# One level of Strassen's scheme for the down projection of two token chunks, and a scale's matmul moved later

## The chip, the cores and the metric

The kernel runs on one core of one Trainium2 chip. The metric is the device time of a whole execution in microseconds (us). Names of engines in the profile: PE is TensorE (PEld its weight loads, which overlap PE), DVE is VectorE, ACT is ScalarE, POOL is GpSimd, SP is the engine that starts most transfers. "Lnnn" is a line of that kernel's own source, so the same operation has other line numbers in the kernel before and in the changed one.

## The reference, cut to what matters

A layer of 2048 tokens and width 1024: layer norm, a dilated local attention and its output projection, then layer norm and a gated feed-forward block with 3584 inner features. The change is in the last step, `h @ w_down`.

```
h  = x + A(layernorm(x))                  # attention, cut
def B(x, w_gate, w_up, w_down):
    g = x @ w_gate                        # (2048, 1024) @ (1024, 3584)
    u = x @ w_up
    return (g * u) @ w_down               # (2048, 3584) @ (3584, 1024)
h2 = h + B(layernorm(h))
```

## The kernel before

The tokens are worked in four chunks of 512. Chunks 0 and 1 go through the feed-forward block one by one. Chunks 2 and 3 go through gate and up together, in 14 "paired blocks", which already use one level of Strassen's scheme there (seven products where the plain way has eight). For that the weights are multiplied by a power of two, so that sums in float16 keep their digits. The power comes from the sum of all absolute values of the gate and up weights: ScalarE sums rows, VectorE adds the row sums, and a matmul with a tile of ones adds over the partitions. `make_scale` does the last two steps at once, ahead of chunk 2's output projection `wo_ln2(2)`:

```python
def make_scale():
    row = small.tile([128, 1], F32, tag="l1row")
    nc.vector.tensor_reduce(row[:], l1[:], mybir.AxisListType.X, ALU.add)
    ...                                                    # cut: rowb = row in bf16
    nc.tensor.matmul(ps[:], lhsT=ones[:], rhs=rowb[:].to_broadcast((128, TC)), start=True, stop=True)
    ...                                                    # cut: five small VectorE operations make s and 1/s
...
hT = ffn1(1, lnT2)
make_scale()
bg.finish(atts[2])
l2, hs2 = wo_ln2(2)
```

The down projection of chunks 2 and 3 is the plain one. `h23` holds the 56 tiles of h (28 feature tiles for each of the two chunks). TensorE makes 4 token tiles x 28 products for each half of the output columns and each chunk; the last group is done tile by tile, its fourth tile in two pieces.

```python
for c, hs in ((2, hs2), (3, hs3)):
    hT = [h23[2 * f + c - 2] for f in range(NF)]
    for hf in range(2):
        ffn2(c, hf, hT, hs)          # 4 tiles x 28 matmuls of 128x512, then 4 additions and stores
```

## Time and profile before

| | before |
|---|---|
| median of the first three runs | 799.41 us (798.01 to 801.58) |
| span of the profiled run | 798.9 us |
| PE, DVE, ACT busy in it | 785.1, 529.2, 304.4 us |
| start of the down projection of chunks 2 and 3 ("the seam") | 698.78 us |
| from the seam to the end | 100.1 us |

A share of busy time says which engine is short of time on average; what a stage is worth is read from the wait that ends last in it. Here TensorE has almost no waits, so each hole in it counts in full. The prediction shows the profile's lines.

### The profile page before, as it was taken

The numbers are of one execution on the slowest core, as the hardware profiler recorded it, in microseconds if no ns is written. First come the engines' busy times: TensorE is split into PE (matmuls) and PEld (weight loads), VectorE is DVE, ScalarE is ACT, GpSimd is POOL, SyncE is SP. The second block draws the span as 40 slices with busy tenths as digits, with TensorE's granted clock in tenths as the row PEclk, the third lists the DMA queues.
The fourth block names the chain that finished last, engine by engine and source line by source line (L and its number), as shares of the span: only waits on it lengthen the run. The fifth ranks groups of instructions, "written<-read, shape, count | busy, mean of one in ns | idle before, by whom it ended". The sixth has DMA issues, their size and how long they took to land.

```text
span 798.9 us, 9984 instructions
## 1 busy us (share of the span) xinstructions
PE 785.1 (98%) x3732; PEld 364.7 (46%) x3802; DVE 529.2 (66%) x606; ACT 304.4 (38%) x649; POOL 150.7 (19%) x160
## 2 busy tenths in 40 slices
PE   8999999999999999999999899999999999999998
PEld 5544444444444444444444344444444444444445
DVE  6629999999899998999989753724444444301111
ACT  4627445313766641026666300025455455500000
POOL 0000000200000200002000010066876876400000
PEclk9999999999999999999999999999999999999999
DMA  7898693987955968767637466523233133556500
GB/s 262 258 234 200 172 268 92 288 249 196 336 189 187 299 228 224 235 236 232 199 107 236 158 174 248 158 80 106 59 100 106 55 104 109 175 191 200 169 27 27
DMA packets 190977, 143.28 MB, mean 179 GB/s; under 512 B 79184, under 2 KB 183760, under 8 KB 188880
## 3 DMA queue, kind: packets, MB, share of 16 engines
q1 hardware_dynamic: 187344, 120.61, 50.4%
q0 software_dynamic: 3584, 22.02, 8.1%
q8 instruction: 30, 0.49, 0.2%
q14 instruction: 19, 0.16, 0.1%
HBM read 114.29 MB, written 22.02 MB: 171 GB/s over the span
## 4 chain that ended last, share of the span: by engine, by line
PE 73%; DVE 22%; issue 2%; SPq 1%; DMA 1%; ACT 1%; DVEq 0%
PE acc L602 21%; PE pg L392 9%; PE pu L392 9%; PE pz L653 6%; PE py L653 6%; PE px L653 6%; PE wo L513 5%; DVE pv L475 4%; DVE prod L432 4%; PE ps L392 3%; PE accl L592 3%; PE pv L653 3%; DVE prod L434 2%; DVE oD L485 2%; DVE pv L483 2%
## 5 line engine op out<-in xcount | busy, mean ns | idle before, releaser
L392 PE MATMUL ps<-lnT,w_qkv 128*128 128x512 bf16 x721 | 159.0, 379 | 1.0 <-ACT sg L303 0.2
L392 PEld LDWEIGHTS <-w_qkv 128*128 128x128 bf16 x736 | 71.9, 98 | 86.3 <-issue 0.5
L392 PE MATMUL pu<-lnT,w_wu 128*128 128x512 bf16 x438 | 105.1, 379 | 0.6
L392 PE MATMUL pg<-lnT,w_wg 128*128 128x512 bf16 x440 | 105.1, 379 | 0.4
L602 PE MATMUL acc<-w_wd,gs 128*128 128x512 bf16 x438 | 96.7, 379 | 0.5
L584 DVE TENSOR_TENSOR h<-acc,h 128x512 bf16<-128x512 f32 x28 | 17.4, 683 | 96.4 <-PE acc L602 96.4
L303 ACT CAST sg<-ps 128x512 bf16<-128x512 f32 x96 | 54.8, 590 | 53.2 <-PE ps L392 48.2
L475 DVE TENSOR_TENSOR pv<-vD,at 128x4096 bf16<-128x4096 bf16 x32 | 72.5, 2287 | 0.3
L432 DVE TENSOR_TENSOR prod<-qD,kD 128x4096 bf16<-128x4096 bf16 x32 | 72.3, 2284 | 0.1
L392 PEld LDWEIGHTS <-w_wu 128*128 128x128 bf16 x448 | 43.9, 98 | 52.8
L392 PEld LDWEIGHTS <-w_wg 128*128 128x128 bf16 x448 | 43.8, 98 | 52.9
L653 PEld LDWEIGHTS <-sw 128*128 128x128 f16 x448 | 43.8, 98 | 52.9
L602 PEld LDWEIGHTS <-gs 128*128 128x128 bf16 x448 | 43.8, 98 | 52.9
L513 PE MATMUL wo<-w_wo,oT 128*128 128x512 bf16 x251 | 57.2, 386 | 0.3
L653 PE MATMUL px<-lnT,ws 128*128 128x512 bf16 x211 | 52.6, 379 | 0.6
L573 ACT CAST us<-pu 128x512 bf16<-128x512 f32 x56 | 33.1, 591 | 50.5 <-PE pu L392 49.3
L653 PEld LDWEIGHTS <-ws 128*128 128x128 f16 x336 | 32.9, 98 | 39.6
L568 ACT CAST gs<-pg 128x512 bf16<-128x512 f32 x56 | 33.1, 590 | 45.9 <-PE pg L392 41.8
L182 ACT ACTIVATE rs<-mv,eps 128x1 f32<-128x1 f32 x32 | 9.5, 295 | 107.6 <-DVE mv L179 103.9
L487 POOL DMA_DIRECT2D od<-oD x4 | 2.2, 542 | 249.9 <-DVE oD L485 162.5
L632 POOL TENSOR_TENSOR sw<-ws 128x512 f16<-128x512 f16 x28 | 32.3, 1152 | 87.5 <-PE acc L602 46.4
L513 PEld LDWEIGHTS <-oT 128*128 128x128 bf16 x256 | 25.4, 99 | 31.4 <-issue 2.3
(140 smaller groups left out, 1027.9 us busy)
## 6 DMA issues: line engine op xcount, KB each, us to landing
w_wd<-in_B_w_down_dram SPq DMA_DIRECT2D x32, 896.0 KB, 5.8
w_wg<-in_B_w_gate_dram SPq DMA_DIRECT2D x14, 1024.0 KB, 6.5
w_wu<-in_B_w_up_dram SPq DMA_DIRECT2D x14, 1024.0 KB, 5.2
w_wo<-in_A_wo_dram SPq DMA_DIRECT2D x8, 1024.0 KB, 7.0
w_pair<-in_B_w_gate_dram SPq DMA_DIRECT2D x14, 512.0 KB, 3.8
w_pair<-in_B_w_up_dram SPq DMA_DIRECT2D x14, 512.0 KB, 4.9
w_qkv<-in_A_wqkv_dram SPq DMA_DIRECT2D x5, 1024.0 KB, 8.6
kd<-sg SPq DMA_DIRECT2D x32, 144.0 KB, 2.8
```

Of the source, the lines that this page charges most:

```text
L303: nc.scalar.copy(sg[:, HB:HB + TC], ps[:])
L392: nc.tensor.matmul(ps[:], lhsT=wt[:, ko, bass.ts(j, 128)], rhs=rhs[:, ko, :], start=(ko == 0), stop=(ko == KO - 1))
L432: nc.vector.tensor_tensor(prod[:, j], qD[:], kD[:, :, o:o + SUB], ALU.mult)
L475: nc.vector.tensor_tensor(pv[:, j], vD[:, :, o:o + SUB], at[:, w, None, :].to_broadcast((128, DH, SUB)), ALU.mult)
L513: nc.tensor.matmul(ps[:], lhsT=oTs[c][:, kk, t, :], rhs=wts["wo", c, hf][:, kk, :], start=(kk == 0), stop=(kk == KO - 1))
L568: nc.scalar.copy(gs[:], pg[:])
L573: nc.scalar.copy(us[:], pu[:])
L584: nc.vector.tensor_tensor(hs[t][:, cols], acc[:], hs[t][:, cols], ALU.add)
L592: nc.tensor.matmul(acc[:], lhsT=hT[f][:, bass.ts(t, 128)], rhs=wts["wd", c, hf, f // 7][:, f % 7, bass.ds(lo, n)], start=(f == 0), stop=(f ...
L602: nc.tensor.matmul(acc[t][:], lhsT=hT[f][:, bass.ts(t, 128)], rhs=wts["wd", c, hf, b][:, j, :], start=(f == 0), stop=(f == NF - 1))
L632: nc.gpsimd.tensor_tensor(sw[:, i, 0], a21, a22, ALU.add)
L653: nc.tensor.matmul(ps[:], lhsT=lhs[:, ko, :], rhs=rhs[:, ko, :], start=(fresh and ko == 0), stop=(ko == 3), skip_group_check=not fresh)
```

## The change

The intent is to save an eighth of TensorE's work in the down projection of chunks 2 and 3. The 2x2 scheme splits h by chunk (rows 1 is chunk 2, row 2 is chunk 3) and by even and odd feature tiles, and `w_down` by even and odd feature rows and by left and right output half. The sums and differences are made by VectorE, and the conversions to float16 ahead of them by VectorE and ScalarE. Since h needs a scale as well, ScalarE sums the absolute values of `w_down` (beside chunk 0's down projection) and of h (in the paired blocks). Separately, the gate and up scale's ones-matmul goes behind `wo_ln2(2)`. In the code `HA` are the four quarters of h in bf16, `HF` the same ones times the scale in float16, `b11` to `b22` the quarters of `w_down` (two tiles each, `dn_b11a` and `dn_b11b` in the profile), `t1` and `t2` sums of those, `S1` a sum of quarters of h, and `ps_x` and `ps_y` the PSUM banks (`dx` and `dy` in the profile). The names that begin with `hq` in the profile are the tiles that hold h. The diff, cut to its core:

```diff
 hT = ffn1(1, lnT2)
-make_scale()
+scale_gu.rows()                    # row sums, VectorE
+scale_d.rows()
 bg.finish(atts[2])
 l2, hs2 = wo_ln2(2)
+scale_gu.total()                   # ones-matmul and the five small operations
+scale_d.total()
 ...
-for c, hs in ((2, hs2), (3, hs3)):
-    ...
-        ffn2(c, hf, hT, hs)
+conv_down(down["b12"])             # VectorE: to f16, two tiles of 128x3584
+add_homes(t1v, Fv("b12"), Fv("b11"), ALU.subtract)      # t1, two sums of 128x3584
+scale_h.rows()
+conv_down(down["b21"])
+for q in range(4):
+    dprod(ps_x[q], q, HA["11"], fcells(down["b11"]), True)     # product 1: 14 matmuls for each q
+    if q == 1:
+        scale_h.total(ps_y[3])
+        ...                                                    # cut: inverse of both scales
+for q in range(4):
+    nc.scalar.activation(ps_y[q][:], ps_x[q][:], ACTF.Copy, scale=sh)
+for k in range(NP):                                            # 28 conversions on VectorE
+    to_f16(HF["22"][k], HA["22"][k], sh)
+    to_f16(HF["21"][k], HA["21"][k], sh)
+...                                                            # cut: 14 on ScalarE, S1 = 14 sums
+for q in range(4):
+    dprod(ps_x[q], q, HA["12"], fcells(down["b21"]), False)    # product 2
+    result(2, q, 0, ps_x[q], scale_d.inv, None)
+    if q == 2:
+        conv_down(down["b22"])
+...                                                            # cut: 28 differences on VectorE
+add_homes(t2v, Fv("b22"), t1v, ALU.subtract)                   # t2
+...                                                            # cut: product 3 (S1 x t1)
+for q in range(4):
+    dprod(ps_y[q], q, HF["11"], cells(t2h), False)             # product 4
+...                                                            # cut: products 5 and 6
+for q, lo, n in ((0, 0, 512), (1, 0, 512), (2, 0, 512), (3, 0, 256), (3, 256, 256)):
+    dprod(ps_y[q], q, HF["12"], fcells(down["b22"]), False, lo, n)    # product 7
+    result(2, q, 1, ps_y[q], inv, p5[q], lo, n)
```

Not shown are the loads of `w_down` for this stage, now made once and not once for each chunk, and the warm-up tile, which moves to another pool.

More of the change, by code (lines that the diff above doesn't have):

```diff
@@ L151 @@
     pair_at = len(stream)
-    for c in (2, 3):
-        stream_wd(c, 0)
-        stream_wd(c, 1)
     wts = {}
@@ L281 @@
     nc.scalar.preload_act_table_set("natural_log_exp_and_others")
-    warm = const.tile([128, 512], BF)
+    warm = t1k.tile([128, TC], BF, tag="t1k", name="warm")
     nc.vector.memset(warm[:], 0.0)
@@ L527, in wo_ln2, with __init__, add, rows @@
         return lnT, hs
-    l1 = const.tile([128, 56], F32)
     ones = const.tile([128, 128], BF)
     nc.vector.memset(ones[:], 1.0)
-    scale = {}
+    class Scale:
+        def __init__(self, name, n):
+            self.name, self.n = name, n
+            self.l1 = const.tile([128, n], F32, name="l1" + name)
+            self.rowb = const.tile([128, 1], BF, name="rowb" + name)
+        def add(self, k, src, junk):
+            nc.scalar.activation(junk, src, ACTF.Abs, accum_out=self.l1[:, k:k + 1])
+        def rows(self):
+            row = small.tile([128, 1], F32, tag="l1row", name="row" + self.name)
+            nc.vector.tensor_reduce(row[:], self.l1[:], mybir.AxisListType.X, ALU.add)
+            nc.vector.tensor_copy(self.rowb[:], row[:])
+        def total(self, ps=None):
+            ps = ps or psum.tile([128, TC], F32, tag="mm", name="l1ps" + self.name)
+            nc.tensor.matmul(ps[:], lhsT=ones[:], rhs=self.rowb[:].to_broadcast((128, TC)), start=True, stop=True)
+            tot = const.tile([128, 1], F32, name="tot" + self.name)
+            nc.vector.tensor_copy(tot[:], ps[:, 0:1])
+            eb = const.tile([128, 1], I32, name="eb" + self.name)
+            nc.vector.tensor_scalar(eb[:], tot[:].bitcast(I32), 0x7F800000, None, ALU.bitwise_and)
+            nc.vector.tensor_scalar(eb[:], eb[:], float(27 << 23), None, ALU.max)
+            sb = const.tile([128, 1], I32, name="sb" + self.name)
+            nc.vector.tensor_scalar(sb[:], eb[:], -1.0, float(266 << 23), ALU.mult, ALU.add)
+            ib = const.tile([128, 1], I32, name="ib" + self.name)
+            nc.vector.tensor_scalar(ib[:], eb[:], float(12 << 23), None, ALU.subtract)
+            self.s, self.inv = sb[:].bitcast(F32), ib[:].bitcast(F32)
@@ L535, in abs_sum @@
+    scale_gu, scale_d, scale_h = Scale("gu", 56), Scale("d", 56), Scale("h", 56)
     def abs_sum(c, b, j):
-        k = 28 * c + 4 * b + j
         wt = wts["wg" if c == 0 else "wu", c, b]
         junk = lnp.tile([128, 2, 512], BF, tag="ln", name=f"junk{c}_{b}_{j}")
-        nc.scalar.activation(junk[:], wt[:, bass.ts(j, 2), :], ACTF.Abs, accum_out=l1[:, k:k + 1])
-    def make_scale():
-        row = small.tile([128, 1], F32, tag="l1row")
-        nc.vector.tensor_reduce(row[:], l1[:], mybir.AxisListType.X, ALU.add)
-        rowb = small.tile([128, 1], BF, tag="l1rowb")
-        nc.vector.tensor_copy(rowb[:], row[:])
-        ps = psum.tile([128, TC], F32, tag="mm", name="l1ps")
-        nc.tensor.matmul(ps[:], lhsT=ones[:], rhs=rowb[:].to_broadcast((128, TC)), start=True, stop=True)
-        tot = const.tile([128, 1], F32)
-        nc.vector.tensor_copy(tot[:], ps[:, 0:1])
-        eb = const.tile([128, 1], I32)
-        nc.vector.tensor_scalar(eb[:], tot[:].bitcast(I32), 0x7F800000, None, ALU.bitwise_and)
-        nc.vector.tensor_scalar(eb[:], eb[:], float(27 << 23), None, ALU.max)
-        sb = const.tile([128, 1], I32)
-        nc.vector.tensor_scalar(sb[:], eb[:], -1.0, float(266 << 23), ALU.mult, ALU.add)
-        ib = const.tile([128, 1], I32)
-        nc.vector.tensor_scalar(ib[:], eb[:], float(12 << 23), None, ALU.subtract)
-        scale["s"], scale["inv"] = sb[:].bitcast(F32), ib[:].bitcast(F32)
@@ L559, in ffn1, with abs_sum_down, abs_sum_h @@
+        scale_gu.add(28 * c + 4 * b + j, wt[:, bass.ts(j, 2), :], junk[:])
+    def abs_sum_down(hf, b, j):
+        junk = lnp.tile([128, 512], BF, tag="ln", name=f"junkd{hf}_{b}_{j}")
+        scale_d.add(28 * hf + 7 * b + j, wts["wd", 0, hf, b][:, j, :], junk[:])
+    def abs_sum_h(n, k, ht):
+        junk = lnp.tile([128, 512], BF, tag="ln", name=f"junkh{n}_{k}")
+        scale_h.add(4 * n + k, ht, junk[:])
     def ffn1(c, lnT):
@@ L587, in ffn2 @@
     def ffn2(c, hf, hT, hs, between={}):
-        if c == NCH - 1 and hf == 1:
-            for t, lo, n in ((0, 0, 512), (1, 0, 512), (2, 0, 512), (3, 0, 256), (3, 256, 256)):
-                acc = psum.tile([128, n], F32, tag="mm", name=f"accl{t}_{lo}")
-                for f in range(NF):
-                    nc.tensor.matmul(acc[:], lhsT=hT[f][:, bass.ts(t, 128)],
-                                     rhs=wts["wd", c, hf, f // 7][:, f % 7, bass.ds(lo, n)],
-                                     start=(f == 0), stop=(f == NF - 1))
-                ffn2_store(c, t, hf, acc, hs, lo, n)
-            return
         acc = [psum.tile([128, 512], F32, tag="mm", name=f"acc{c}_{hf}_{t}") for t in range(4)]
@@ L604, in ffn2 @@
                                      start=(f == 0), stop=(f == NF - 1))
+                if c == 0:
+                    abs_sum_down(hf, b, j)
                 bg.step(0.86)
@@ L626, in weight_sums @@
         wt = wpool.tile([128, KO, 2, 256], F16, tag="w", name=f"ws_{n}")
-        nc.vector.tensor_scalar(wt[:], raw[:], scale["s"], None, ALU.mult)
+        nc.vector.tensor_scalar(wt[:], raw[:], scale_gu.s, None, ALU.mult)
         sw = wpool.tile([128, 2, 4, 4, 128], F16, tag="w", name=f"sw_{n}")
@@ L654, in product, with pair_block @@
                              stop=(ko == 3), skip_group_check=not fresh)
-    def pair_block(n, hts):
+    def pair_block(n, hts, sums=()):
         b11, b21, t1, t2, t3, t4, b22 = pair["b"]
-        wt, sw, inv = pair["a", n], pair["s", n], scale["inv"]
+        wt, sw, inv = pair["a", n], pair["s", n], scale_gu.inv
         gu = range(2)
@@ L683, in pair_block @@
             nc.scalar.activation(out[i][0], xb[i][:], ACTF.Copy, scale=inv)
+            for k in sums[2 * i:2 * i + 2]:
+                k()
         for i in gu:
@@ L758, with home, load_down, to_f16 @@
         h23 += [ht[:, k, :] for k in range(KO)]
+    wd_e = B_w_down.rearrange("(n e p) c -> e p n c", e=2, p=128)
+    NH = NF // 4
+    def home(pool, tag, name, dt=F16):
+        return pool.tile([128, KO, TC], dt, tag=tag, name=name)
+    def load_down(homes, e, hf):
+        for a, t in enumerate(homes):
+            nc.sync.dma_start(t[:, 0:NH, :], wd_e[e][:, bass.ts(a, NH), bass.ts(hf, 512)])
+    def to_f16(dst, src, sc, eng=nc.vector):
+        if eng is nc.scalar:
+            nc.scalar.activation(dst, src, ACTF.Copy, scale=sc)
+        else:
+            eng.tensor_scalar(dst, src, sc, None, ALU.mult)
+    def f16(ap):
+        return ap.bitcast(F16)
+    def conv_down(homes):
+        for t in homes:
+            to_f16(f16(t[:, 0:NH, :]), t[:, 0:NH, :], scale_d.s)
+    def cells(homes):
+        return [t[:, k, :] for t in homes for k in range(NH)]
+    down = {}
     for n in range(NP):
@@ L763 @@
                 load_pair(n + 2)
-        else:
-            state["limit"] = len(stream)
-            pump()
-        pair_block(n, h23[4 * n:4 * n + 4])
-    pump()
-    for c, hs in ((2, hs2), (3, hs3)):
-        hT = [h23[2 * f + c - 2] for f in range(NF)]
-        for hf in range(2):
-            ffn2(c, hf, hT, hs)
+            else:
+                names = ("b11a", "b12a", "b21a", "b21b", "b12b")
+                ws = {k: home(wpool, "w", "dn_" + k, BF) for k in names}
+                down["b11"] = [ws["b11a"], home(att, "oD", "dn_b11b", BF)]
+                down["b12"] = [ws["b12a"], ws["b12b"]]
+                down["b21"] = [ws["b21a"], ws["b21b"]]
+                load_down(down["b11"], 0, 0)
+                load_down(down["b12"], 0, 1)
+        else:
+            load_down(down["b21"], 1, 0)
@@ new lines @@
+        sums = [] if n == 0 else [
+            (lambda n=n, k=k: abs_sum_h(n - 1, k, h23[4 * (n - 1) + k])) for k in range(4)]
+        pair_block(n, h23[4 * n:4 * n + 4], sums)
+        if n == NP - 2:
+            conv_down(down["b11"])
+    HA = {"11": h23[0::4], "21": h23[1::4], "12": h23[2::4], "22": h23[3::4]}
+    for k in (3, 0, 2, 1):
+        abs_sum_h(NP - 1, k, h23[4 * (NP - 1) + k])
+    down["b22"] = [home(wpool, "w", "dn_b22a", BF), home(wpool, "w", "dn_b22b", BF)]
+    load_down(down["b22"], 1, 1)
@@ new lines, with add_homes, dprod @@
+    t1h = [home(lnTp, "lnT", "dn_t1a"), home(lnTp, "lnT", "dn_t1b")]
+    t2h = [home(att, "kD", "dn_t2a"), home(att, "vD", "dn_t2b")]
+    Fv = lambda k: [f16(t[:, 0:NH, :]) for t in down[k]]
+    def add_homes(dst, x0, x1, op):
+        for d, a0, a1 in zip(dst, x0, x1):
+            nc.vector.tensor_tensor(d, a0, a1, op)
+    ps_x = [psum.tile([128, TC], F32, tag="mm", name=f"dx{q}") for q in range(4)]
+    ps_y = [psum.tile([128, TC], F32, tag="mm", name=f"dy{q}") for q in range(4)]
+    def dprod(ps, q, lhs, rhs, fresh, lo=0, n=TC):
+        for k in range(NP):
+            nc.tensor.matmul(ps[:, bass.ds(lo, n)], lhsT=lhs[k][:, bass.ts(q, 128)], rhs=rhs[k][:, bass.ds(lo, n)],
+                             start=(fresh and k == 0), stop=(k == NP - 1), skip_group_check=not fresh)
@@ new lines, in fcells, with result @@
+    def fcells(homes):
+        return [f16(c) if c.dtype != F16 else c for c in cells(homes)]
+    def result(c, q, hf, ps, sc, other, lo=0, n=TC):
+        rows = (hs2 if c == 2 else hs3)[q]
+        cols = bass.ds(hf * 512 + lo, n)
+        nc.vector.scalar_tensor_tensor(rows[:, cols], ps[:, bass.ds(lo, n)], sc,
+                                       rows[:, cols] if other is None else other[:, bass.ds(lo, n)], ALU.mult, ALU.add)
+        nc.sync.dma_start(outf[bass.ds(c * TC + q * 128, 128), cols], rows[:, cols])
@@ new lines @@
+    conv_down(down["b12"])
+    t1v = [t[:, 0:NH, :] for t in t1h]
+    t2v = [t[:, 0:NH, :] for t in t2h]
+    add_homes(t1v, Fv("b12"), Fv("b11"), ALU.subtract)
[5 more added lines that the diff above has]
+            scale_h.total(ps_y[3])
+            inv = const.tile([128, 1], F32, name="inv_hd")
+            nc.vector.tensor_tensor(inv[:], scale_h.inv, scale_d.inv, ALU.mult)
+            inv = inv[:]
@@ new lines @@
+    sh = scale_h.s
+    for q in range(4):
+        nc.scalar.activation(ps_y[q][:], ps_x[q][:], ACTF.Copy, scale=sh)
+    HF = {k: [f16(a) for a in HA[k]] for k in HA}
+    for k in range(NP):
+        to_f16(HF["22"][k], HA["22"][k], sh)
+        to_f16(HF["21"][k], HA["21"][k], sh)
+    s1h = [t[:, 0:NH, :] for t in down["b11"]]
+    S1 = fcells(down["b11"])
+    for k in range(NP):
+        to_f16(HF["11"][k], HA["11"][k], sh, nc.scalar)
+    for k in range(NP):
+        nc.vector.tensor_tensor(S1[k], HF["21"][k], HF["22"][k], ALU.add)
@@ new lines @@
+    for q in range(4):
[3 more added lines that the diff above has]
+            conv_down(down["b22"])
+    for k in range(NP):
+        nc.vector.tensor_tensor(HF["21"][k], HF["11"][k], HF["21"][k], ALU.subtract)
+    for k in range(NP):
+        nc.vector.tensor_tensor(HF["11"][k], S1[k], HF["11"][k], ALU.subtract)
+    add_homes(t2v, Fv("b22"), t1v, ALU.subtract)
+    p5 = []
+    for q in range(4):
+        dprod(ps_x[q], q, S1, cells(t1h), True)
+        p = lnp.tile([128, TC], F32, tag="ln", name=f"dp5_{q}")
+        nc.scalar.activation(p[:], ps_x[q][:], ACTF.Copy, scale=inv)
+        p5.append(p)
@@ new lines @@
+    add_homes(Fv("b12"), Fv("b22"), Fv("b12"), ALU.subtract)
+    add_homes(Fv("b21"), Fv("b21"), t2v, ALU.subtract)
+    for q in range(4):
+        dprod(ps_y[q], q, HF["11"], cells(t2h), False)
+        nc.scalar.copy(ps_x[q][:], ps_y[q][:])
+    for k in range(NP):
+        to_f16(HF["12"][k], HA["12"][k], sh, nc.scalar)
+    for q in range(4):
+        dprod(ps_x[q], q, HF["21"], fcells(down["b12"]), False)
+        r = att.tile([128, TC], F32, tag=("lg", "t3")[q % 2], name=f"dr{q}")
+        nc.vector.tensor_tensor(r[:], p5[q][:], hs3[q][:, 512:1024], ALU.add)
+        result(3, q, 1, ps_x[q], inv, r)
@@ new lines @@
+    for k in range(NP):
+        nc.vector.tensor_tensor(HF["12"][k], HF["12"][k], HF["11"][k], ALU.subtract)
+    for q in range(4):
+        nc.vector.tensor_tensor(p5[q][:], p5[q][:], hs2[q][:, 512:1024], ALU.add)
+    for q in range(4):
+        dprod(ps_x[q], q, HF["22"], fcells(down["b21"]), False)
+        result(3, q, 0, ps_x[q], inv, None)
+    for q, lo, n in ((0, 0, 512), (1, 0, 512), (2, 0, 512), (3, 0, 256), (3, 256, 256)):
+        dprod(ps_y[q], q, HF["12"], fcells(down["b22"]), False, lo, n)
+        result(2, q, 1, ps_y[q], inv, p5[q], lo, n)
```

## The prediction

> **What bounds the kernel now.** I read the page's busy line and its row of slices first, then who TensorE waited for, then stretches of the span where something waits, then the groups with shapes kept apart.
>
> ```profile
> PE 785.1 (98%) x3732; PEld 364.7 (46%) x3802; DVE 529.2 (66%) x606; ACT 304.4 (38%) x649; POOL 150.7 (19%) x160
> PEclk9999999999999999999999999999999999999999
> ...
> PE l1ps L547 <- DVE rowb L545: 3.7, 1, 3.7
> PE ps L354 <- DMA w_qkv<-in_A_wqkv_dram: 1.4, 2, 0.9
> ```
>
> TensorE is busy 785.1 of 798.9 us: it is the bound everywhere, so only two things can shorten the kernel, fewer matmul columns or fewer holes. The list of TensorE's waits (last two lines) has one hole worth naming: the ones-matmul that sums the weight scale waits 3.7 us for VectorE's row sum, which stands behind the attention in VectorE's order. What that hole costs is seen in six stretches around it (columns: stretch, us, busy of PE, PEld, DVE, ACT, POOL, granted clock, DMA share, GB/s):
>
> ```profile
> 448.00:452.00 4.00, 0.35 (x2) 0.17 (x2) 3.59 (x5) 1.63 (x3) 0.40 (x1) 0.97 0.85 275
> 452.00:453.00 1.00, 1.00 (x4) 0.43 (x3) 0.65 (x5) 0.00 (x0) 0.16 (x1) 0.50 1.07 378
> 453.00:454.00 1.00, 1.00 (x4) 0.30 (x3) 0.03 (x1) 0.00 (x0) 0.00 (x0) 0.50 1.04 354
> 454.00:455.00 1.00, 1.00 (x4) 0.30 (x3) 0.00 (x0) 0.00 (x0) 0.00 (x0) 0.50 1.09 447
> 455.00:456.00 1.00, 1.00 (x6) 0.47 (x5) 0.48 (x1) 0.00 (x0) 0.00 (x0) 0.89 1.00 426
> 456.00:458.00 2.00, 2.00 (x11) 0.93 (x10) 0.96 (x3) 0.00 (x0) 0.00 (x0) 1.00 0.25 102
> ```
>
> After the hole TensorE is busy but granted 0.50 of its clock up to 455, then all of it. Half speed lasts some 3.46 us (0.03 x 4 / 0.5 = 0.24, then 3.00, then 0.11 / 0.5 = 0.22), which loses 1.73 us. The hole costs 3.65 + 1.73 = **5.4 us**.
>
> The stages that the change touches are the down projection of chunk 0 (302.8 to 351.2), the paired blocks (530 to 698.8), and the down projection of chunks 2 and 3 (from 698.8 on):
>
> ```profile
> 302.80:351.20 48.40, 48.14 (x221) 21.94 (x225) 45.99 (x39) 2.05 (x5) 0.00 (x0) 1.00 0.68 217
> 530.00:698.80 168.80, 168.06 (x770) 76.54 (x783) 75.85 (x123) 89.59 (x140) 117.11 (x104) 1.00 0.35 106
> 698.80:798.90 100.10, 96.48 (x469) 46.47 (x475) 12.47 (x22) 0.00 (x1) 0.00 (x0) 1.00 0.38 122
> ```
>
> In the last one VectorE (12.47 us) and ScalarE (0.00) are idle: the change spends this idle time. The unit prices are in these groups:
>
> ```profile
> L436 DVE TENSOR_TENSOR prod<-prod 128x2048 bf16<-128x2048 bf16 x16 | 19.6, 1223 | 0.4
> L627 DVE TENSOR_SCALAR ws<-w_pair,sb 128x4096 f16<-128x4096 bf16 x14 | 17.9, 1280 | 0.0
> L690 DVE TENSOR_TENSOR hq<-hq,up 128x512 bf16<-128x512 bf16 x24 | 8.5, 418 | 0.0
> L187 DVE TENSOR_SCALAR ln<-h,mv,rs 128x1024 bf16<-128x1024 bf16 x16 | 8.8, 551 | 2.7 <-ACT rs L183 2.4
> L539 ACT ACTIVATE junk<-w_wu 128x1024 bf16<-128x1024 bf16 x28 | 29.7, 1061 | 0.0
> ...
> 698.98 0.75 DVE L688 SCALAR_TENSOR_TENSOR up<-py,ib,p 128x512 bf16<-128x512 f32 x1 [0.97 <-PE py L653]
> 699.65 1.42 DVE L690 TENSOR_TENSOR hq_p<-hq_p,up 128x512 bf16<-128x512 bf16 x4
> ```
>
> A 16-bit sum of two tiles takes 0.418 us for 512 and 1.223 for 2048 elements, so 2.02 for the new 3584; one that follows another starts 0.08 us before its end (0.34 and 1.95 in a row). The f16 conversion of 4096 takes 1.28; between it and the 1024 of L187 the slope is 0.238 ns, so 3584 takes 1.16 (1.09 in a row) and 512 some 0.43 (0.355 in a row) at most. The last two lines, from the timeline, place VectorE at the seam: its h products end at 701.07, 2.3 us after the down projection has begun (698.78).
>
> **What the Trainium skill says.** "TensorE: Matmul & The Clock Gate", part 1, has the clock fall to one half after an idle window of about 3.4 us and come back after a busy one; its start-to-start for 512 columns is 215.7 ns warm. The trace agrees: 3.65 us idle, 3.46 us at 0.50, and matmuls every 0.216 us. "VectorE: DVE Perf Modes", what auto-detection checks, lets a one-source 16-bit op in SBUF run four wide, and caps a two-source one at two wide: 1280 ns against 2284 ns (group of L432) for 4096 elements agrees. "ScalarE: Activation LUTs", what ACT_TABLE_LOAD costs, gives 186 ns + 0.833 ns an element, each pointer operand 93 ns more, with back-to-back overlap of 93 ns: 1061 ns here for 1024 (1039 by the page). So 512 absolute values are an estimate of 0.61 us, plus the 0.19 of the accumulator read: 0.81 a pair in sequence, as 1.24 for 1024 now less 0.43. A conversion of 512 with a pointer scale is an estimate of 0.61 in a row.
>
> **Part by part.** *Removed:* the down projection has 2 chunks x 2 halves x 4 tiles x 28 = 448 matmuls of 512 columns. Seven products x 4 x 14 are 392. 56 x 0.216 = **12.1 us** less on TensorE. Its 14.7 MB of weight loads become 7.3, hidden before and after.
>
> *Moved:* the scale's matmul goes behind the output projection of chunk 2, by when VectorE has long made the row sum. Nothing else makes TensorE wait there: the projection takes 8 banks that ScalarE has emptied, VectorE starts on them at some 452.1 (TensorE would have the eighth at 461.9) and the next stage needs the third bank at 462.3, free at about 456. The whole 5.4 returns, less 0.2 for a second ones-matmul and 0.1 in rounding: **5.1 us**. Attention 3's result is stored from 451.6 whatever happens, and is used 16 us after it landed, so it doesn't take the gain.
>
> *Added on ScalarE:* 56 absolute sums beside the down projection of chunk 0, 56 x 0.81 = 45.4 us. It is free from 308 (earlier work waits for VectorE), so it ends at about 356 rather than 353 where its next copies start now; VectorE first needs one of them at 357.4. Free. In the paired blocks 4 x 0.81 = 3.2 us are added to 89.59 / 14 = 6.4 us, in a block of 12.06: about 9.6, free.
>
> *Added at the end,* in us from the seam T0. VectorE is in strict order: products to 2.3; convert b12 to 4.5; t1 = b12 - b11, two sums, to 8.5; row sum, 0.46 until the matmul can start as now. TensorE wants that at 28 x 0.216 = 6.05 and gets it at 8.9: **stall 2.85**. The first product ends at 15.2, the second at 27.3 (ScalarE's copies with the scale are ready from 12.6). VectorE then converts b21 and makes the scale (to 12.0), converts 28 tiles of h (9.9, to 22.0), makes S1 (14 x 0.34, to 26.8), three results (28.9), b22 (31.0) and the fourth result (31.7). The third product needs the first result's bank at 27.6: **stall 0.3**; it ends at 39.7. For the fourth VectorE has yet to do 28 differences (9.6, to 41.3) and t2 (two sums, the first at 43.3, the second at 45.2): **stall 3.7 + 0.4**. With cheaper small conversions (0.27) it is 1.7 less, so 3.3 on average. From there VectorE and ScalarE stay ahead: b12 and b21 differences to 53, one product lasts 12.1, and HF12 is ready 6 us before the last product. The tail is the same as now. Two holes of about 3 us may also throw the clock to one half, at 1.7 each: 2.85 is under the window and 3 to 4 is around it, so I charge 0.8 of one, 1.4.
>
> Sum at the end: 12.1 - 0.2 (scale of h) - 2.85 - 0.3 - 3.8 - 1.4 = 3.5. With 5.1: **8.6 us**, 799.4 - 8.6 = **790.8 us**.
>
> **The rivals.** (1) TensorE stays the bound all along: no stalls, 12.1 + 5.1 - 0.2 = 17.0, so 782.4, just over 2%. For it: order of work looks arranged for it (b22's conversion stands between results, ScalarE takes 28 of the conversions). Against it: two full-size sums stand ahead of the row sum, and 28 differences plus two sums in VectorE's order between products 3 and 4, 13.5 us plus leftovers against 12.1. (2) VectorE becomes the bound of the first half of the stage, small ops cost more than their slopes say, and both holes throttle: stalls 9 to 10 and 3.4 of half clock, nothing left of the 12.1; the moved matmul alone gives 794 to 795. (3) ScalarE's sums hold weight buffers or attention and make TensorE wait in chunk 0's stage: 45 us in 48 is tight, buffers come free 5 to 7 us later than now; against it, seven tiles of prefetch, each 6 us of TensorE. It would cost 1 to 4 us. (4) The gain of the moved matmul is hidden by a later wait; I find none.
>
> **Range and chances.** The moved matmul is nearly certain; the stalls' sum runs from 3 to 10 and the clock from 0 to 3.4. That gives 786 to 796. Over 2% faster means under 783.4, which needs nearly no stall: 0.06. Over 2% slower would need a mechanism that I don't see: 0.02.
>
> **What would show it.** The wait for the row sum gone at 448, no 0.50 clock there, chunk 2's projection starting 3.7 us earlier; one TensorE hole of about 3 us in the middle of the first product, before the ones-matmul, and one of 3 to 4 us ahead of the fourth product, released by VectorE; 392 matmuls at 0.216 us. Wrong if the holes are absent (then nearer 783), if the clock falls twice (794), or if TensorE waits in chunk 0's down projection or the paired blocks.

## The result, and the profile after

The changed kernel takes 787.83 us (median of 4 runs, 787.08 to 789.03), the kernel before 799.16 (4 runs, 798.01 to 801.58). The ratio is 0.9856, with a 95% interval of 0.9828 to 0.9883. Ratios here are the mean time of one kernel's runs over that of the other's of the same rounds, so they are not quite the ratios of the medians quoted. The gain is 11.3 us, where 8.6 was predicted.

The page of the changed kernel and who TensorE waited for (waiting operation, releaser, us in total, times, longest):

```profile
PE 773.4 (98%) x3672; PEld 358.1 (46%) x3734; DVE 586.5 (75%) x729; ACT 394.8 (50%) x913; POOL 150.8 (19%) x160
...
PE dy L547 <- DVE rowbh L543: 2.5, 1, 2.5
...
PE dy L840 <- DVE h L849: 0.6, 1, 0.6
PE dy L840 <- DVE dn_t2a L833: 0.6, 1, 0.6
...
PE dy L840 <- DVE dn_t2b L833: 0.3, 1, 0.3
```

PE's busy time fell by 11.7 us, VectorE took on 57 us and ScalarE 90. The wait of 3.7 us is gone. Four new waits on VectorE stand in the new stage. The stretches around the old hole, and the three stages again (us, busy of PE, PEld, DVE, ACT, POOL, clock, DMA share, GB/s):

```profile
448.00:452.00 4.00, 4.00 (x21) 1.80 (x19) 3.93 (x8) 0.82 (x2) 0.56 (x1) 1.00 0.87 291
452.00:456.00 4.00, 4.00 (x20) 1.82 (x19) 3.96 (x9) 0.50 (x2) 0.00 (x0) 1.00 0.95 370
...
301.95:350.35 48.40, 48.14 (x221) 21.96 (x225) 45.99 (x39) 36.36 (x117) 0.00 (x0) 1.00 0.73 218
529.00:692.61 163.61, 162.87 (x746) 74.17 (x759) 75.17 (x121) 115.14 (x239) 115.11 (x103) 1.00 0.38 108
692.61:785.40 92.79, 85.67 (x408) 39.68 (x406) 67.51 (x136) 27.27 (x49) 0.00 (x0) 1.00 0.13 43
```

TensorE is now full where the hole was, at full clock. Chunk 0's down projection takes 48.4 us as before, though ScalarE works 36.4 us in it and not 2.1. The last stage is 92.8 us, not 100.1: 7.3 less. It begins at 692.61 rather than 698.78, 6.2 earlier; 0.5 of that is the first loads of the run (the first full group of the QKV projection starts at 16.95 here and at 17.47 in the trace before), so 5.7 is the moved matmul.

Where the 7.3 comes from is seen in the timelines of the last stage, first TensorE's where it waited, then VectorE's (start, us, operation, count, idle time before it and releaser):

```profile
698.22 0.59 PE L840 MATMUL dx<-dn_b11b,hq_p 128*128 128x512 f16 x2
701.26 0.39 PE L547 MATMUL dy<-rowbh,ones 128*128 128x512 bf16 x1 [2.45 <-DVE rowbh L543]
...
732.42 1.46 PE L840 MATMUL dy<-dn_t2a,hq 128*128 128x512 f16 x6 [0.55 <-DVE dn_t2a L833]
...
734.36 0.38 PE L840 MATMUL dy<-dn_t2b,hq_h 128*128 128x512 f16 x1 [0.26 <-DVE dn_t2b L833]
...
780.44 0.81 PE L840 MATMUL dy<-dn_b22a,hq 128*128 128x256 f16 x6 [0.58 <-DVE h L849]
```

```profile
693.48 1.42 DVE L700 TENSOR_TENSOR hq_p<-hq_p,up 128x512 bf16<-128x512 bf16 x4
694.81 1.15 DVE L789 TENSOR_SCALAR dn_b12a<-dn_b12a,sbd 128x3584 f16<-128x3584 bf16 x1
...
698.88 2.02 DVE L833 TENSOR_TENSOR dn_t1b<-dn_b12b,dn_b11b 128x3584 f16<-128x3584 f16 x1
700.81 0.20 DVE L542 TENSOR_REDUCE rowh<-l1h 128x1 f32<-128x56 f32 x1
...
704.15 3.24 DVE L789 TENSOR_SCALAR hq<-hq,sbh 128x512 f16<-128x512 bf16 x12
707.30 1.14 DVE L789 TENSOR_SCALAR hq_h<-hq_h,sbh 128x512 f16<-128x512 bf16 x4
...
730.36 2.01 DVE L833 TENSOR_TENSOR dn_t2a<-dn_b22a,dn_t1a 128x3584 f16<-128x3584 f16 x1
732.29 2.01 DVE L833 TENSOR_TENSOR dn_t2b<-dn_b22b,dn_t1b 128x3584 f16<-128x3584 f16 x1
```

No line of VectorE in this stretch of the timeline, shown or cut, has idle time before it: from the h products at 693.48 to the end of t2 at 734.3 it never rests (the view marks idle time over 0.15 us), and three of TensorE's holes end where it delivers the row sum and the two parts of t2. The fourth hole is in the last product: the right half of the fourth token tile waits until VectorE has read the left half, which lies in the same bank.

A hole is 0.16 us longer than the idle time shown, because a matmul's modelled 379 ns reach past the 216 ns after which the next could start. With that the stage adds up: 56 x 0.2157 = 12.08, less 0.22 for the scale's matmul, less (2.45 + 0.55 + 0.26 + 0.58 + 4 x 0.16 = 4.48) is 7.38; measured 7.3.

### The profile page after: what moved, and what is told of

It reads as the page before. It is cut to its first block, busy times and chain, and to the rows that moved or that the text cites. A ratio compares the mean times of both kernels' runs of the same rounds, so it can differ in the third digit from the quotient of the medians.

```text
span 785.4 us, 10283 instructions
## 1 busy us (share of the span) xinstructions
PE 773.4 (98%) x3672; PEld 358.1 (46%) x3734; DVE 586.5 (75%) x729; ACT 394.8 (50%) x913; POOL 150.8 (19%) x160
## 4 chain that ended last, share of the span: by engine, by line
PE 75%; DVE 21%; issue 1%; SPq 1%; DMA 1%; ACT 0%; DVEq 0%
PE pu L389 12%; PE acc L608 12%; PE pg L389 12%; PE pz L661 6%; PE py L661 6%; PE px L661 6%; PE wo L510 5%; DVE prod L429 4%; PE ps L389 3%; PE dx L840 3%; PE pv L661 3%; PE dy L840 3%; DVE pv L472 2%; DVE prod L431 2%; SPq L223 1%
## 5 line engine op out<-in xcount | busy, mean ns | idle before, releaser
L510 PE MATMUL wo<-w_wo,oT 128*128 128x512 bf16 x251 | 55.6, 379 | 0.3
L431 DVE TENSOR_TENSOR prod<-prod 128x4096 bf16<-128x4096 bf16 x16 | 36.6, 2288 | 0.3
```

The costliest lines, as they stand in the source:

```text
L431: nc.vector.tensor_tensor(prod[:, :, 0:16], prod[:, :, 0:16], prod[:, :, 16:32], ALU.add)
L510: nc.tensor.matmul(ps[:], lhsT=oTs[c][:, kk, t, :], rhs=wts["wo", c, hf][:, kk, :], start=(kk == 0), stop=(kk == KO - 1))
```

## The experiments

Ten runs, all correct, each timed in five rounds against the kernel before. The runs of the kernel before had medians of 800.46, 800.15 and 800.75 us in the three sets. Two things make comparison sharper than the medians. The time of the first loads differs by up to 1.4 us between profiles, so I also give the length of the last stage in the profile, from the seam to the end. And each run lists its mean granted clock: mostly 1.000, 0.998 or 0.996. The mean counts time in which TensorE is idle as well, so it is a sign of half clock and not a measure of the time lost.

### The changed kernel again

No edit.

> The changed kernel once more, for its spread on one chip. Expected 787 to 789 us. Theory of the two clock states: its 2.45 us hole in the first product sometimes throws TensorE to half clock for one stretch of about 3.4 us, so runs fall into two groups some 1.7 us apart, with mean granted clock 1.000 and 0.998. Rival: the spread is plain noise of loads, and clock and time aren't linked.

Measured: 788.37 us (787.80 to 789.05), ratio 0.985. With the four runs of the result there are eight: four at clock 1.000, with a mean of 787.5, and four at 0.998, with 788.8. Clock and time go together, so the two groups are real, 1.3 us apart where 1.7 was expected. Two later traces show why it is less: with half clock after this hole (the runs "undone" and "last pieces alone" below) TensorE comes later to the fourth product, and the wait of 0.55 us for t2's first part is no longer in their lists. The kernel before has the same groups, and a third one; over its 27 runs of the three sets:

| clock of the run | 1.000 | 0.998 | 0.996 |
|---|---|---|---|
| runs | 4 | 13 | 10 |
| mean us | 798.49 | 800.36 | 801.49 |

A deficit of 0.002 over 800 us is 3.2 us at half clock, about the one stretch that the prediction read from the trace; 0.004 is twice that time. So the hole of the kernel before is followed by none, one or two such times, from run to run. There is a trace for one of its runs only, with one.

What decides whether the clock falls can be read from the twelve traces. In each, the time from one change of the clock to the next is a whole multiple of 3.413 us (447.15, 3.41 and 344.75 us in the kernel before are 131, 1 and 101 of them), and where the program's start lies in this beat differs from trace to trace: the first change of the clock comes between 4.27 and 7.22 us. Cut at this beat, the two traces nearest to each other look like this:

```profile
700.12:703.54 3.42, 1.64 (x8) 0.80 (x9) 3.39 (x5) 0.00 (x0) 0.00 (x0) 1.00 0.01 5
703.54:706.95 3.41, 3.41 (x18) 1.54 (x16) 3.27 (x16) 1.82 (x3) 0.00 (x0) 1.00 0.00 0
...
730.54:733.96 3.42, 1.29 (x7) 0.58 (x6) 3.42 (x3) 0.00 (x0) 0.00 (x0) 1.00 0.00 0
733.96:737.37 3.41, 3.39 (x9) 1.16 (x8) 3.41 (x3) 0.00 (x0) 0.00 (x0) 0.50 0.00 0
```

The first two lines are of this run: TensorE is idle for 1.78 us of a window, and the next one has full clock. The last two are of the run with the row sum earlier, below: idle for 2.12 us, and the next window has half. All holes of over 1 us in the middle of the kernel:

| trace | hole, us | most idle time in one window, us | clock of the next |
|---|---|---|---|
| changed, and its repeat | 2.45, 2.44 | 1.50, 1.78 | full |
| conversions on ScalarE, no down sums | 2.45, 2.45 | 1.47, 1.60 | full |
| row sum earlier | 3.15 | 2.12 | half |
| undone (two holes) | 3.65, 2.44 | 2.27, 2.23 | half |
| last pieces alone | 2.45 | 2.34 | half |
| row sum later | 4.57 | 2.34, then 2.23 | half, then half |
| before | 3.65 | 3.29 | half |

So in these traces it is not the hole's length that counts but how much of it falls into one window; the border lies between 1.78 and 2.12 us. As an estimate with the border at 2.1 and the beat's place left to chance, half clock follows a hole of 2.45 us in (3.41 + 2.45 - 4.2) / 3.41 = 49% of runs and one of 3.65 in 84%. By their mean clock it was 9 of 21 (the changed kernel and the three variants with this hole) and 23 of 27.

### The moved matmul, undone and alone

Undone, in the changed kernel:

```diff
 scale_gu.rows()
+scale_gu.total()
 scale_d.rows()
 bg.finish(atts[2])
 l2, hs2 = wo_ln2(2)
-scale_gu.total()
 scale_d.total()
```

> The changed kernel with the gate and up scale's ones-matmul back ahead of chunk 2's output projection. If the hole of 3.65 us and its half clock of 1.73 us came back whole, the time is 5.1 to 5.5 us above the changed kernel (about 793), the hole is in the list of waits again, and the clock is 0.998 in every run. Rival, that the later part hides the delay: less than 2 us above it.

Measured: 794.55 us (794.20 to 794.81), 6.2 above the changed kernel of the same set and not 5.1 to 5.5, clock 0.996 in all five runs and not 0.998. The profile shows where the rest lies. The seam comes 681.13 us after the first QKV group, in the changed kernel 675.66: 5.5 later, as expected of the hole. The other 1.2 us are in the last stage (93.97 us against 92.77), where this run has half clock after the row sum's hole too. Its two large waits:

```profile
PE l1psgu L547 <- DVE rowbgu L543: 3.7, 1, 3.7
PE dy L547 <- DVE rowbh L543: 2.4, 1, 2.4
```

Alone, in the kernel before: `make_scale` is cut in two, the row sum stays ahead of the projection and the ones-matmul goes behind it.

```diff
-make_scale()
+make_rows()
 bg.finish(atts[2])
 l2, hs2 = wo_ln2(2)
+make_scale()
```

> The kernel before with nothing but the ones-matmul moved behind chunk 2's output projection, its row sum staying where it was. Theory: 5.1 to 5.5 us below the kernel before, about 794, clock 1.000. Then the Strassen part alone is worth the other 6 us of the 11.4. Rival, that the two parts are not additive: 0 to 3 us.

Measured: 794.74 us (794.23 to 794.90), 5.7 below the kernel before, ratio 0.9928, clock 1.000 in four runs and 0.999 in one. So the moved matmul is worth 5.7 us, and the Strassen part the remaining 6.4 (794.74 to 788.37). Together that is 12.1 and not the 11.3 of the result, since the four runs of the kernel before had a median of 799.16 there and have 800.46 in this set. The parts are additive to within the clock states, and nothing later hides the first. Against the kernel before at clock 1.000 (four runs of the three sets) the mean of these runs (794.65) is 3.84 lower: about the bare hole, 3.65 + 0.16. The remaining 1.9 us are the half clock, in its average over runs.

### The row sum earlier

```diff
 conv_down(down["b12"])
+scale_h.rows()
 add_homes(t1v, Fv("b12"), Fv("b11"), ALU.subtract)
-scale_h.rows()
```

> The changed kernel with the row sum of the h scale put ahead of the two t1 sums in VectorE's order, nothing else. Theory A, VectorE's queue from the seam up to t2 is the bound (39.8 us against 36.5 of TensorE): the hole of 2.45 in the first product goes, the hole ahead of the fourth product grows from 0.55 to about 3.0, the time stays within 0.5 us of the changed kernel. Rival B, the row sum's place costs its own 2.45 us: the time falls by 2.4 us and the fourth product's hole stays under 1.

Measured: 788.74 us (787.33 to 789.17), ratio 0.9847. The two runs at clock 1.000 have 787.4, the changed kernel's in the same set 787.9; the three at 0.998 have 788.9, as its own. The wait for the row sum is gone and this one has grown from 0.6:

```profile
PE dy L840 <- DVE dn_t2a L833: 3.1, 1, 3.1
```

Theory A holds, B falls. Taking away a wait of 2.45 us on the path gave 0.5 us at full clock and nothing at 0.998, because the same engine is late again 31 us further on: one hole of 3.15 + 0.16 = 3.3 stands in place of three that sum to 2.45 + 0.55 + 0.26 + 3 x 0.16 = 3.7. VectorE's queue from the seam to t2 sets the time here, and where TensorE waits for it makes little difference.

### Conversions on ScalarE

```diff
-def conv_down(homes):
+def conv_down(homes, eng=nc.vector):
     for t in homes:
-        to_f16(f16(t[:, 0:NH, :]), t[:, 0:NH, :], scale_d.s)
+        to_f16(f16(t[:, 0:NH, :]), t[:, 0:NH, :], scale_d.s, eng)
...
-conv_down(down["b21"])
+conv_down(down["b21"], nc.scalar)
...
-            conv_down(down["b22"])
+            conv_down(down["b22"], nc.scalar)
```

> The changed kernel with the f16 conversions of b21 and b22 on ScalarE (about 3.2 us each tile there, in its idle stretches) and not on VectorE, the row sum where it was. VectorE is relieved of 4.3 us after the row sum. Both theories: the hole of 2.45 in the first product stays, the holes of 0.55 and 0.26 in the fourth go: 0.8 us below the changed kernel, about 787.0.

Measured: 786.70 us (786.57 to 788.58), ratio 0.9834. Its waits in the stage:

```profile
PE dy L547 <- DVE rowbh L543: 2.4, 1, 2.4
PE dy L840 <- DVE h L849: 0.6, 1, 0.6
PE dy L840 <- DVE dn_t2b L833: 0.3, 1, 0.3
```

The last stage of its profile is 784.8 - 692.47 = 92.3 us, 0.5 below the changed kernel. The expectation was 0.8: the wait for t2's first part went, that for its second part stayed, though VectorE has 4.3 us less to do. The last result of product 2 stands in VectorE's order ahead of the differences and can't be made before TensorE has finished that product (VectorE waits 2.27 us for it here, at 719.68), so this end of the queue no longer depends on how early VectorE is.

### Both, and the order of the last pieces

Both edits together:

> Both: row sum early, and the conversions of b21 and b22 on ScalarE. Theory A: now VectorE's queue (39.8 - 4.3 = 35.5 us) is shorter than TensorE's 36.5, so all three holes go, 3.3 us below the changed kernel in the same clock state, and as no hole is left the clock is 1.000 in every run: about 784. Rival B, that each of the two parts has its own separate worth: the sum of what the two single runs give.

Measured: 784.85 us (784.58 to 785.22), ratio 0.9805, clock 1.000 in three runs and 0.999 in one. The last stage of its profile is 782.8 - 693.15 = 89.65 us: 3.15 below the changed kernel. By rival B the sum of the single edits would have been 0.4 + 0.5. So the two edits are worth much only together: one moves the first deadline out of VectorE's way, the other shortens the queue ahead of the second. The wait of 0.3 us for t2's second part stayed, as in the run before, so two of the three holes went. With no hole over 0.6 us left in the stage the half clock is gone behind it. (The 0.999 of one run would be 1.6 us at half clock. It may lie after the last matmul, which ends 3.2 us before the end of the profile; no trace shows it.)

Then with the pieces of the last product in another order:

```diff
-for q, lo, n in ((0, 0, 512), (1, 0, 512), (2, 0, 512), (3, 0, 256), (3, 256, 256)):
+for q, lo, n in ((3, 0, 256), (0, 0, 512), (1, 0, 512), (2, 0, 512), (3, 256, 256)):
     dprod(ps_y[q], q, HF["12"], fcells(down["b22"]), False, lo, n)
```

> As the run before, and in the last product the left half of the fourth tile goes first rather than next to last, so that its right half doesn't wait for VectorE to have read the same bank. Expected: the hole of 0.58 us in the last product goes, 0.5 to 0.6 us below the run before, about 783.4, the best of all.

Measured: 783.24 us (782.70 to 783.92), ratio 0.9788 with an interval of 0.9769 to 0.9807, the best of all; the interval reaches over 0.98, so the record calls it unclear whether it is 2% faster. Its last stage is 780.9 - 691.99 = 88.9 us, 0.7 below the run before it, near the 0.58 + 0.16 of the hole; the other 0.9 us between the medians is more than this edit can give, and the profiles of the two differ by 1.2 in their first loads. The only wait left in the stage is the one for t2's second part:

```profile
PE dy L840 <- DVE dn_t2b L833: 0.3, 1, 0.3
```

### The row sum later

The hole is made longer, with VectorE's work as it is:

```diff
-scale_h.rows()
 conv_down(down["b21"])
+scale_h.rows()
```

> The changed kernel with the row sum put behind the conversion of b21 on VectorE: 2.1 us later, VectorE's total work unchanged. Theory A: the hole in the first product is 4.6 us, those of the fourth product go, holes in all 4.6 against 3.3, and a hole over 3.4 us always brings the half clock: 1.3 plus 1.7, so 3.0 above the changed kernel's fast group, about 790, with clock 0.998 in every run. Rival, that the clock doesn't depend on the hole's length: 1.3 above, clock 1.000 in some runs.

Measured: 790.53 us (790.15 to 791.64), ratio 0.9878; clock 0.998 in two runs and 0.996 in two, never 1.000. The hole and the clock after it in its profile:

```profile
PE dy L547 <- DVE rowbh L543: 4.6, 1, 4.6
...
697.18:700.59 3.41, 1.07 (x5) 0.29 (x3) 3.41 (x3) 0.00 (x0) 0.00 (x0) 1.00 0.27 86
700.59:707.42 6.83, 4.59 (x11) 1.64 (x12) 5.95 (x22) 1.24 (x2) 0.00 (x0) 0.50 0.00 0
```

The clock falls at 700.59, within the hole, stays at 0.50 past its end at 702.83, and comes back at 707.42. So 0.996 is here not two separate falls but one stretch of two windows, for 2.24 us of which TensorE was idle anyway. The time is 3.0 above the changed kernel's group at full clock (787.5), as expected, but not by the sum expected: the last stage of the profile is 96.65 us, 3.9 above the changed kernel's, which is 2.12 of longer hole, 4.59 / 2 = 2.3 of half clock and 0.55 less for t2's first part; the first loads were 0.5 us shorter. The wait for t2's second part stayed. The rival, no link between the hole's length and the clock, falls: no run has 1.000.

### The sums that were added on ScalarE

The 56 absolute sums of the down weights are left out and a constant takes their place, for the time alone:

```diff
+nc.vector.memset(scale_d.l1[:], 12.0)
...
-if c == 0:
-    abs_sum_down(hf, b, j)
```

> The changed kernel without the 56 absolute sums of the down weights on ScalarE; the scale comes from a constant of the right size, so this is for the time alone. If ScalarE's added 45 us beside chunk 0's down projection are free, as the prediction has it: within 0.3 us of the changed kernel. Rival: they hold weight buffers or VectorE's attention, then it is 1 to 4 us faster.

Measured: 788.71 us (786.97 to 789.39), ratio 0.9848; one run at clock 1.000, three at 0.998 (mean 788.9, the changed kernel's 788.8). The seam is 675.6 us after the first QKV group (692.43 - 16.82), in the changed kernel 675.7 (692.61 - 16.95). The sums cost nothing. They take 34.3 us of ScalarE and not the predicted 45.

### The order of the last pieces alone

The edit of the last pieces in the changed kernel, nothing else.

> The changed kernel with nothing but the order of the last product's pieces changed (left half of the fourth tile first). The hole of 0.58 us lies on the path to the end and nothing hides it: 0.5 to 0.6 us less. Rival: the last piece then waits for something else and the time stays.

Measured: 787.27 us (787.01 to 788.38), ratio 0.9832. The wait is gone from its list. Four runs are at clock 1.000 (mean 787.2), against 787.5 for the changed kernel's four, which are from other sets of runs: a difference of 0.3, too near to the spread of the first loads to confirm 0.6 by the time alone. The length of the last stage does confirm it. Its profile is of the run at 0.998, and the profile with the move undone has the same last stage in the old order, also with one window of half clock after the row sum's hole: 93.97 us there and 93.17 here, 0.8 less, against the hole's 0.58 + 0.16. The profile also shows half clock behind a hole of only 2.45 us:

```profile
PE dy L547 <- DVE rowbh L543: 2.4, 1, 2.4
...
701.95:705.36 3.41, 3.30 (x8) 1.19 (x9) 3.27 (x11) 0.49 (x1) 0.00 (x0) 0.50 0.00 0
```

## Why the prediction was right or wrong

The time lies in the range (787.83 in 786 to 796), the change is within 2% as was held most likely, and the mechanism was the one foretold: holes of the new stage, released by VectorE, take back part of the 12.1 us. The gain came out 2.7 us larger. By steps:

- **Saved matmul columns, 12.1 us:** right. 7 x 56 matmuls every 0.216 us.
- **Moved matmul, 5.1 us:** it gave 5.7, shown both by doing it alone and by its trace. The hole is 3.81 with the 0.16 that the idle time leaves out, and the half clock averages 1.9 over the runs of the kernel before (none in 4 of 27, twice the time in 10) where I took the single trace's 1.73. The 5.1 had 0.2 taken off for a second ones-matmul, which that run doesn't have; like for like it is 5.5.
- **Added sums on ScalarE, free:** right, shown by leaving the larger part of them out; beside the part in the paired blocks no wait of TensorE is listed. The price of a pair was too high, 0.81 us: 56 of them keep ScalarE busy for 34.3 us, 0.61 each. In the trace each operation starts 0.09 us before the one ahead of it has ended, the accumulator's reads too, and the prediction took nothing off for that.
- **First hole, 2.85 us at the row sum:** right in place and cause; 2.45 idle, 2.6 from start to start.
- **Hole ahead of the third product, 0.3:** not there; S1 and the results were early.
- **Hole ahead of the fourth product, 3.7 + 0.4, charged as 3.8:** this is the term that failed. It was 0.55 + 0.26 idle, 1.1 with the 0.16 each. I priced the small conversions at 0.355 us in a row, on a line through an operation with two pointer operands (L187); these have one and take 0.263:

```profile
L789 DVE TENSOR_SCALAR hq<-hq,sbh 128x512 f16<-128x512 bf16 x12 | 3.2, 347 | 0.0
```

  (3.15 us from the first of the 12 to the next group.) That is 28 x 0.092 = 2.6 us of VectorE's queue, and with 0.5 at its head and 0.4 in sums and results it reached t2's first part at 39.8 and not at 43.3. The prediction did name the cheaper price, but put its effect at 1.7 where 28 x 0.085 is 2.4, called the average hole 3.3 and then took 3.8 into the sum. Both slips went the same way.
- **Half clock in the new stage, 1.4 us charged:** the profiled run has none; half of the changed kernel's runs have one stretch, 1.3 us, so 0.7 on average. That it came at all is partly luck: the prediction expected it mainly of a hole of 3 to 4 us ahead of the fourth product, and it came after the first hole, which the prediction had put under the window.
- **Not foreseen:** 0.58 us in the last product. The kernel before splits its last tile over two banks, the changed one over two halves of one bank, since it adds onto what stands there. "PSUM — Partial Sum Buffer", the section on bank collisions, has the rule to guard PSUM by bank and not by address; the trace shows such a guard (TensorE waits 0.58 us for VectorE's read of the other half), and putting the halves apart in time took the wait away. Both halves are also one tile of the program, and no run tells the bank from the tile.

In sum at the end of the kernel: predicted 12.1 - 0.2 - 2.85 - 0.3 - 3.8 - 1.4 = 3.5; measured 12.1 - 0.2 - 2.6 - 1.1 - 0.75 - 0.7 = 6.7 in the average run. The two medians 794.74 and 788.37 say 6.4; another 0.2 is the ones-matmul of the down weights' scale, which the second kernel has as well.

Of the rivals, the first (no holes, 782.4) is what the changed kernel could have been: with three edits it is 783.24. The second, both holes at full size and both with half clock, did not come. What is open: where exactly between 1.78 and 2.12 us of idle time in a window the half clock sets in, and what the runs of the kernel before at 0.996 look like, of which there is no trace.

## What to carry to other kernels

When work moves from the bound engine to an idle one, add up the helper's queue between two deadlines rather than its share of the span: here VectorE was busy without a rest for 41 us inside a stage in which it was idle for a quarter of the time. A wait that such a queue causes can't be removed by reordering alone (0.4 us for the reorder, 0.5 for the shortened queue, 3.15 for both). And a hole in TensorE is dearer than it looks, by the half clock behind it: 3.65 us of idle time cost 5.7 on average.

## What the Trainium skill lacked or had wrong

- "TensorE: Matmul & The Clock Gate", part 1, ties the fall of the clock to an idle window of about 3.4 us that runs freely. The traces here agree on the length (3.413 us) and on the free run. But the window need not be idle throughout: half clock followed windows with 2.12 to 3.29 us of idle time, and none with 1.78 or less. So a hole of 2.45 us is no safety, and one of 3.65 no certainty (none in 4 of 27 runs, going by the mean clock of 1.000).
- The same page, under its terms, puts the loss at half of the time at half clock. One window is 1.7 us by that, and the groups of the kernel before lie 1.9 apart. In the changed kernel it cost 1.2 to 1.3, because a later wait took part of it; and of the 6.83 us in the run with the row sum later, TensorE was idle for 2.24.
- "VectorE: DVE Perf Modes" gives a fixed cost per instruction, but no page gives the price of a second pointer operand there: a conversion of 512 elements with one takes 347 ns, and 263 in a row, while a straight line through 1024 elements with two (551 ns) and 4096 with one (1280 ns) puts it at 430. The operation with two pointers also does two steps of arithmetic, and no run separates the two.
- "ScalarE: Activation LUTs" was right on both sizes used: 612 ns for 512 absolute values (its formula: 613), 709 ns for a conversion with a pointer scale (its formula: 706). No page gives the price of reading the accumulator: 186 ns by itself, and nothing on top in a row, since 56 pairs took 34.3 us.
